# A light convolution with a maxout layer on one core: the chunk with the partitions' first tokens goes last, and the opening's weight work is laid out anew

## The chip, the cores and the metric

The kernel runs on one core of a Trainium2 chip. The metric is the device time of one execution in microseconds (us), taken as the median of several runs. The engines are called as the profile calls them: PE is TensorE's matrix multiply and PEld its loading of weights, DVE is VectorE, ACT is ScalarE, POOL is GpSimd, SP is SyncE, which issues most of the DMA transfers. L802 is line 802 of the kernel's file; the kernel before and the changed one have line numbers of their own.

## The reference

Eight sequences of 4160 tokens with 192 channels are convolved along the sequence. Each token has its own seven taps for each of eight heads of 24 channels; the taps go through a softmax first. The sequence is padded with six zero rows at its front. Then each of the 33,280 tokens goes through a maxout layer of 768 features and back to 192 channels.

```
w = exp(weight_gen - max(weight_gen)); w = w / (sum(w) + 1e-9)          # over the 7 taps
conv[b, s, head, g] = sum over k of w[b, s, head, k] * x_pad[b, s + k, head, g]
h = maximum(maximum(conv @ w1, conv @ w2), conv @ w3)                   # 192 -> 768
out = h @ w_out                                                          # 768 -> 192
```

The four weight matrices arrive as 64-bit floats, the rest is 32-bit.

## The kernel before, in words

**Layout.** The 33,280 tokens lie on 128 partitions, 260 consecutive tokens to each, 16 partitions to a sequence. A *chunk* is four tokens of every partition, 512 tokens, so there are 65 chunks. Chunks are loaded in *supers*: chunk 0 alone, then pairs (1, 2), (3, 4) and so on. A super brings two pieces: the taps `wt` and the tokens `xt`, which have six more tokens ahead of the first one for the convolution; each of the two has two buffers. Those six lie in the same partition's row of the input, except at a partition's first tokens, where they are the last of the partition before, or zeros at a sequence's start. So `load_super` treats the supers with a partition's first six tokens (chunk 0, and chunk 1 with two of them) in another way: a memset of zeros on DVE and eight short transfers, one for each sequence (L305, half of chunk 0's on ACT's queue).

**A chunk's way.** *Softmax* of the taps, once per super: maximum (DVE, L326), difference (POOL, L331), exponential (ACT, L335), sum (DVE, L340), 1e-9 added (DVE, L344), reciprocal (DVE, L348), product (POOL, L352). *Taps*: for each of the four tokens of a partition one product of 128 x 1344 elements on POOL (L370, into one of three buffers `r`) and one sum over the seven taps on DVE (L382, into `acc`). *Turn*: channels must come to the partitions; for chunks 0 and 1 PE transposes (L402, L403), for the later ones DVE transposes 32 x 32 blocks (L421) and 24 ACT copies put them in place (L432). *Parts*: each value is split in a rounded high part and the rest, and the products of the parts together come near 32-bit precision (`xa_hi` L444 and `xc` L449 on ACT, `xa_lo` L460 and `xb` L465 on POOL, for the first two chunks on DVE).

**Products.** The maximum of three is taken as conv @ w1 plus the maximum of 0, conv @ (w2 - w1) and conv @ (w3 - w1). So a chunk has twelve *groups up* (six blocks of 128 features, two differences each), nine matmuls of 64 rows each (L802), and four *groups down* with 30 matmuls each (also L802). Groups down multiply by w_out and, for the w1 term, by w1 @ w_out (`wca`, `wcb`), which `compose` makes once from turned pieces of w1 (`turn_weights` L731 and L733; `compose` L750). Each group has a lower and an upper half of PE's rows; after the last matmul of a lower half an empty instruction stands in SP's queue (L808), and the upper half of that group starts only after it.

**Weights.** `single` makes 32-bit floats out of the 64-bit words in five passes, one on ACT (L573) and four on DVE (L579, L586, L595, L604), the first into a PSUM bank. It does so fifteen times, for nine pieces of 256 elements per partition and six of 384. `prepare_a` and `prepare_b` then take the differences (POOL, L631 and L661), their high parts (ACT) and low parts (POOL, L643 and L673); `prepare_down` does the like for w_out.

**The order.** All instructions are put in order by `Plan` when the program is built, and each engine runs its instructions in that order (`pin`). A task has an engine, a cost, things that must be done before it, buffers that it holds (`holds`, counted against each pool) and a due time. The plan plays the program through: when an engine is free, the ready task with the earliest due time goes next if its buffers are free. Only PE's two queues, L and U, keep the order in which they were written. The due times before are set by hand:

```
    def needed(c):
        return FIRST + PERIOD * c
    ...
        due = needed(cs[0]) - 40
```

The loop writes the chunks in order: twelve groups up of a chunk, with the groups down of the chunk before in the middle; `compose` comes after the first six groups up of chunk 1, and the turns of w1 after chunk 0's groups up.

Of the kernel before, what the change touches and what calls it, by code (L numbers as in the profile page):

```python
# [17 lines left out]
P = 128  # L18


class Hold:


    def __init__(self, pool):
        self.pool, self.users, self.taken, self.tile = pool, 0, False, None


class Task:
    def __init__(self, engine, cost, emit, deps, due, holds, end):
# [11 lines left out]
class Plan:  # L41
# [4 lines left out]
    LATENCY = 0.12  # L46

    def __init__(self, pools):
        self.free = dict(pools)
        self.waiting = {"L": [], "U": []}  # L50
        self.tasks = []

    def add(self, engine, cost, emit, deps=(), due=0.0, holds=(), end=None):
# [3 lines left out]
        if engine in self.FIXED:  # L57
            self.waiting[engine].append(t)
        return t

    def order(self):
        ready, busy, events, done = {}, {}, [], []
        at = dict.fromkeys(self.FIXED, 0)
        for t in self.tasks:
            ready.setdefault(t.engine, [])
            busy.setdefault(t.engine, 0.0)
            if t.missing == 0 and t.engine not in self.FIXED:
                heapq.heappush(ready[t.engine], (t.due, t.n, t))

        def can(t):  # L70
            need = {}
            for h in t.holds:
                if not h.taken:
                    need[h.pool] = need.get(h.pool, 0) + 1
            return all(self.free[p] >= n for p, n in need.items())

        def start(t, now):
            for h in t.holds:
                if not h.taken:
                    h.taken = True  # L80
                    self.free[h.pool] -= 1
# [3 lines left out]
            heapq.heappush(events, (now + t.cost, 0, t.n, t, "free"))  # L85
            heapq.heappush(events, (now + t.end, 1, t.n, t, "given"))
            heapq.heappush(events, (now + t.end + self.LATENCY, 2, t.n, t, "seen"))

        now = 0.0
        while True:  # L90
            for e in ready:
                if busy[e] > now + 1e-9:
                    continue
                if e in self.FIXED:
                    k = at[e]
                    if k < len(self.waiting[e]):
                        t = self.waiting[e][k]
# [33 lines left out]
def lightconv_maxout_kernel(  # L131
# [31 lines left out]
    ON_POOL = (1, 4)  # L163

# [15 lines left out]
    halves = (slice(0, DB), slice(DB, P))  # L180

# [9 lines left out]
    w1a = const.tile([P, NJ, P], F32, name="w1a")  # L191
    b32 = const.tile([P, NP, 3, P], F32, name="b32")
# [39 lines left out]
    plan = Plan(counts | {"conv": 3})  # L232
# [14 lines left out]
    def vec(n):  # L247
        return 0.15 + 0.00105 * n

    def act(n):  # L250
        return 0.18 + 0.00084 * n

    def gps(n):
        return 0.1 + 0.0024 * n


    PERIOD = 21.0
    FIRST = 22.0
# [14 lines left out]
    def load_super(s):  # L273
        cs = supers[s]
        a, n = cs[0] * TC, len(cs) * TC
        hx, hw = xts[s], wts[s] = hold("xt"), hold("wt")
        due = needed(cs[0]) - 40

# [753 lines left out]
```

## Time and profile before

| | |
|---|---|
| median of 3 runs | 1444.12 us (1441.09 to 1446.23) |
| the profiled execution | 1444.6 us |
| its span on the core | 1442.8 us |
| PE busy | 1402.0 us, 97% of the span |
| ACT busy | 1117.3 us, 77% |
| POOL busy | 1104.2 us, 77% |
| DVE busy | 1043.4 us, 72% |
| mean granted PE clock | 0.987 |
| moved by DMA | 85.08 MB, 59 GB/s on the mean |

The shares are means over the whole span, and the stages differ: in the first slices PE is busy for 2 to 8 tenths, then for 9 or more to the end. What a change in the opening is worth is thus read from the opening's own rows (busy time by stretch, what each instruction waited for), and what it does to the rest from a stretch of the rest. A row of the chain of waits gives the start and the length of an instruction, its engine, line, operation, output and inputs, and in brackets how long the engine had waited for it and for what. A row of a group gives the count, the busy time, the mean length in ns and the idle time ahead of it with what ended most of it.

### The profile page before, as it was taken

The numbers are of one execution on the slowest core, as the hardware profiler recorded it, in microseconds if no ns is written. First come the engines' busy times: TensorE is split into PE (matmuls) and PEld (weight loads), VectorE is DVE, ScalarE is ACT, GpSimd is POOL, SyncE is SP. The second block draws the span as 40 slices with busy tenths as digits, with TensorE's granted clock in tenths as the row PEclk, the third lists the DMA queues.
The fourth block names the chain that finished last, engine by engine and source line by source line (L and its number), as shares of the span: only waits on it lengthen the run. The fifth ranks groups of instructions, "written<-read, shape, count | busy, mean of one in ns | idle before, by whom it ended". The sixth has DMA issues, their size and how long they took to land.

```text
span 1442.8 us, 37119 instructions
## 1 busy us (share of the span) xinstructions
PE 1402.0 (97%) x14878; PEld 1366.1 (95%) x14878; DVE 1043.4 (72%) x1433; ACT 1117.3 (77%) x2828; POOL 1104.2 (77%) x609
## 2 busy tenths in 40 slices
PE   2889999999999999999999999999999999999999
PEld 1579999999999999999999999999999999999998
DVE  7867777777777787777778777877877677777543
ACT  3547878878877887787788778877888887788773
POOL 6769888778877887887788778778877877787421
PEclk9679999999999999999999999999999999999999
DMA  7102111111111111111011111101111111110000
GB/s 249 46 1 79 57 68 57 68 68 57 68 46 46 57 68 68 68 57 64 28 57 68 68 68 57 68 25 67 57 68 68 57 68 44 48 57 24 23 21 26
DMA packets 23405, 85.08 MB, mean 59 GB/s; under 512 B 2768, under 2 KB 9544, under 8 KB 19136
## 3 DMA queue, kind: packets, MB, share of 16 engines
q1 hardware_dynamic: 23112, 82.44, 15.5%
q8 instruction: 116, 1.90, 0.5%
q14 instruction: 57, 0.47, 0.1%
q10 hardware_dynamic: 120, 0.28, 0.1%
HBM read 57.15 MB, written 25.56 MB: 57 GB/s over the span
## 4 chain that ended last, share of the span: by engine, by line
PE 95%; POOL 1%; DMA 1%; ACT 1%; SPq 1%; DVE 1%; issue 0%; POOLq 0%
PE bank L802 95%; POOL r L370 1%; DMA xt<-in_x_dram 1%; SPq L532 1%; DVE den L344 0%; ACT room L432 0%; DMA raw<-in_moe_w_dram 0%; SPq L516 0%; PE bank L733 0%; ACT m L859 0%; POOL wa_lo L643 0%; PE bank L731 0%; ACT wb_hi L684 0%; DVE acc L382 0%; ACT bank L573 0%
## 5 line engine op out<-in xcount | busy, mean ns | idle before, releaser
L370 POOL TENSOR_TENSOR r<-xt,wt 128x1344 f32<-128x1344 f32 x260 | 727.1, 2845 | 143.2 <-DVE acc L382 142.9
L802 PE MATMUL bank<-wo,h_hi 64*128 64x384 f32 x3120 | 675.0, 357 | 0.0
L802 PE MATMUL bank<-wo,h_lo 64*128 64x192 f32 x3120 | 603.4, 249 | 0.0
L432 ACT COPY room<-room 32x128 f32<-32x128 f32 x1512 | 448.4, 297 | 79.0 <-DVE room L421 55.9
L802 PEld LDWEIGHTS bank<-wo,h_lo 64*128 64x128 f32 x3120 | 493.0, 188 | 0.0
L802 PEld LDWEIGHTS bank<-wo,h_hi 64*128 64x128 f32 x3120 | 489.2, 186 | 0.0
L802 PE MATMUL bank<-xa_hi,wa_hi 64*128 64x512 f32 x1560 | 479.9, 394 | 6.0 <-ACT wa_hi L637 3.4
L802 PE MATMUL bank<-xa_hi,wa_lo 64*128 64x512 f32 x1560 | 477.9, 390 | 3.4 <-POOL wa_lo L643 3.3
L802 PE MATMUL bank<-xa_lo,wa_hi 64*128 64x512 f32 x1560 | 476.8, 391 | 0.5 <-DVE xa_lo L460 0.5
L382 DVE TENSOR_REDUCE acc<-r 128x192 f32<-128x1344 f32 x260 | 399.8, 1538 | 0.6 <-POOL r L370 0.3
L859 ACT ACTIVATE m<-bank 128x512 f32<-128x512 f32 x390 | 234.5, 601 | 71.4 <-PE bank L802 66.7
L935 DVE TENSOR_TENSOR o<-bank,ob 128x192 f32<-128x192 f32 x260 | 92.4, 356 | 268.7 <-ACT ob L928 268.5
L802 PE MATMUL bank<-xb,wb_hi 64*128 64x512 f32 x780 | 284.5, 390 | 0.3 <-DVE xb L465 0.3
L802 PE MATMUL bank<-xc,wb_hi 64*128 64x512 f32 x780 | 281.1, 390 | 0.2 <-ACT wb_hi L684 0.2
L802 PEld LDWEIGHTS bank<-xa_hi,wa_hi 64*128 64x128 f32 x1560 | 255.3, 186 | 13.5 <-ACT wa_hi L637 4.3
L802 PEld LDWEIGHTS bank<-xa_hi,wa_lo 64*128 64x128 f32 x1560 | 255.3, 186 | 11.2 <-POOL wa_lo L643 5.6
L802 PEld LDWEIGHTS bank<-xa_lo,wa_hi 64*128 64x128 f32 x1560 | 254.9, 187 | 6.4 <-DVE xa_lo L460 1.5
L802 PE MATMUL bank<-xc,wb_lo 64*128 64x512 f32 x780 | 258.0, 389 | 0.0
L867 DVE TENSOR_TENSOR bank<-bank,m 128x512 f32<-128x512 f32 x260 | 179.0, 689 | 42.2 <-PE bank L802 24.3
L878 POOL TENSOR_TENSOR h_lo<-m,h_hi 128x512 fp32r<-128x512 f32 x130 | 171.7, 1321 | 40.0 <-ACT h_hi L871 39.9
L802 PE MATMUL bank<-wca,xa_hi 64*128 64x384 f32 x520 | 183.4, 353 | 0.0
L878 DVE TENSOR_TENSOR h_lo<-bank,h_hi 128x512 fp32r<-128x512 f32 x260 | 172.4, 681 | 11.4 <-ACT h_hi L871 11.2
(79 smaller groups left out, 2012.5 us busy)
## 6 DMA issues: line engine op xcount, KB each, us to landing
xt<-in_x_dram SPq DMA_DIRECT2D x31, 1344.0 KB, 5.8
out_dram<-o SPq DMA_DIRECT2D x64, 384.0 KB, 2.3
wt<-in_weight_gen_dram SPq DMA_DIRECT2D x32, 224.0 KB, 2.6
h_hi<-in_moe_w_dram SPq DMA_DIRECT2D x6, 256.0 KB, 2.9
xt<-in_x_dram SPq DMA_DIRECT2D x1, 1152.0 KB, 5.8
h_lo<-in_moe_w_dram SPq DMA_DIRECT2D x6, 128.0 KB, 4.0
raw<-in_moe_w_dram SPq DMA_DIRECT2D x3, 256.0 KB, 3.6
room<-in_moe_w_out_dram SPq DMA_DIRECT2D x2, 384.0 KB, 6.4
```

The lines of the kernel that those rows point to most:

```text
L370: nc.gpsimd.tensor_tensor(buf(hr).rearrange("p (h g) k -> p k h g", g=G), buf(hx)[:, la + t : la + t + K].rearrange("p k (h g) -> p k h g" ...
L382: pin(nc.vector.tensor_reduce(buf(ha)[:, t], buf(hr), axis=AX.X, op=ALU.add))
L432: pin(nc.scalar.copy(to[:, :, p : p + 32], b[p : p + 32, :, f : f + 32]))
L532: nc.sync.dma_start(out=raw_b()[h, jps[0] : jps[-1] + 1, i].rearrange("p j n w -> p j (n w)"), in_=w[P:].rearrange("p (j o n) -> p j o n", ...
L802: ins = nc.tensor.matmul(buf(hb)[:, :n], w()[h], v()[h], start=half == 0 and first, stop=half == 1 and last,)
L859: lambda: pin(nc.scalar.activation(buf(hm), buf(hb), AF.Relu)), [made], due,
L867: lambda: pin(nc.vector.tensor_tensor(buf(keep), buf(hb), buf(hm), op=ALU.max)),
L878: eng.tensor_tensor(buf(hl)[:, j], buf(keep), buf(hh)[:, j].bitcast(F32), op=ALU.subtract)
L935: nc.vector.tensor_tensor(buf(ho)[:, t], buf(hb)[:, :D], buf(hq), op=ALU.add)
```

## The change: what it does

**The chunk order.** A table `place` says which tokens position c of the program works on: positions 0 to 62 take chunks 2 to 64, and the last two take chunks 0 and 1. The partitions' first tokens are thus in the last super. Their border rows come by four strided transfers (L357) in place of eight per super.

**The opening.** A list `OPENING` writes out loads, softmax, conversions, taps, turns, differences, groups up, compose and groups down for the first two positions; from position 2 on the loop is as before. On PE's queue all turns of both positions' tokens and of w1 now stand ahead of the first group up, and groups of both positions alternate; compose comes after six groups.

**Engines of the weight work.** A table `MODE` says per difference whether POOL or PE makes it (a product with the identity less one with w1, "L") and which engine takes the low part. Both differences of a piece may be one instruction. Ten of the fifteen clamps of `single` go from DVE to POOL, into one of the buffers `m`.

**Single steps.** Two of the first eight tap products go from POOL to DVE; for positions 0 and 1 POOL makes the low parts of h of three blocks of six, not of two; the 1e-9 of every softmax is added on ACT.

**The plan.** Due times may be left out; each task then gets the latest start that the tasks after it allow (`start_by`). Costs are fitted anew, and at most eight transfers are in flight at a time. Loads, softmax and taps from the third super on keep due times, now counted from PE's planned clock.

```diff
+    def start_by(self):
+        for t in reversed(self.tasks):
+            latest = [a.by - self.LATENCY - t.end for a in t.after]
+            if t.due is not None:
+                latest.append(t.due)
+            t.by = min(latest, default=1e6)
...
+    ON_POOL_FIRST = (1, 2, 4)
+    TAPS_ON_VECTOR = ((0, 2), (1, 2))
+    MODE = {
+        ("a", 0): ("POOL", "POOL"),
+        ("a", 1): ("L", "DVE"),
+        ("a", 2): ("POOL", "DVE"),
+        ("b", 0): ("POOL", "POOL"),
+        ("b", 1): ("POOL", "POOL"),
+        ("b", 2): ("POOL", "DVE"),
+    }
+    CLAMP_ON_POOL = (("a", 0, 1), ("a", 1, 1), ("a", 1, 2), ("a", 2, 0), ("a", 2, 1), ("b", 0), ("b", 1), ("b", 2), ("d", 0), ("d", 2),)
...
+    place = [*range(2, NC), 0, 1]
...
+    OPENING = (
+        ("load", 0), ("load a", 0), ("load b",), ("load a", 1), ("load", 1), ("load a", 2),
+        ("load down",), ("softmax", 0), ("softmax", 1), ("singles", 0), ("singles", 1),
+        ("singles", 2), ("singles down",), ("taps", 0), ("taps", 1), ("turn x", 0, 0),
...
+        ("a", 2, 0, 2), ("b", 1), ("b", 2), ("turn", 2), ("parts", 1), ("b", 0), ("up", 0, 0),
+        ("up", 0, 5), ("up", 1, 0), ("compose",), ("up", 0, 2), ("up", 1, 1), ("up", 0, 4),
+        ("up", 0, 1), ("up", 0, 3), ("up", 1, 5), ("up", 1, 4), ("down", 0), ("up", 1, 2),
+        ("up", 1, 3),
+    )
...
-    plan = Plan(counts | {"conv": 3})
+    plan = Plan(counts | {"conv": 3, "flight": 8})
...
-        a, n = cs[0] * TC, len(cs) * TC
+        a, n = place[cs[0]] * TC, len(cs) * TC
...
-        due = needed(cs[0]) - 40
+        due = clock[0] - 31 if s > 1 else LOAD_DUE["s", s]
...
+            step = 2
+            while step <= PB:
+                def rows(step=step):
+                    to = buf(hx)[step // 2 :: step, :z]
+                    of = xf[step // 2 - 1 :: step, NT - z :][: P // step]
+                    pin(nc.sync.dma_start(out=to, in_=of))
...
         e = plan.add(
-            "DVE", 0.3, lambda: pin(nc.vector.tensor_scalar_add(part(hd), part(hd), 1e-9)),
-            [d], due + 3, [hd],
+            "ACT", 0.25,
+            lambda: pin(nc.scalar.activation(part(hd), part(hd), AF.Copy, bias=1e-9)),
+            [d], due(3), [hd],
...
+            eng, cost = ("DVE", vec(D * K)) if (c, t) in TAPS_ON_VECTOR else ("POOL", 2.6)
...
+    def difference(shape, w, of, deps, holds, on):
...
+        def mult():
+            wide = buf(hb)[:, : n * m]
+            pin(nc.tensor.matmul(wide, ident, w().rearrange("p i n -> p (i n)"), start=True, stop=False))
+            for i in range(n):
+                pin(nc.tensor.matmul(wide[:, i * m : (i + 1) * m], minus, of(), start=False, stop=i == n - 1))
```

The order of the instructions on three engines shows where this puts them. The names in it are the buffers with their number; "waits" names the semaphores of an instruction by the engine or the DMA queue that raises them.

SP's queue in the opening, before, from the first transfer of w_out (`room`) to the first store of results:

```order
L552 DMA room_236<-in_moe_w_out_dram 128x2x384 [waits DMAHW1_49]
L552 DMA room_236<-in_moe_w_out_dram 128x2x384 [waits DMAHW2_49]
L552 DMA h_lo_156<-in_moe_w_out_dram 128x2x384 [waits DMAHW3_49]
L280 DMA wt_248<-in_weight_gen_dram 128x448 [waits DMAHW4_49,Pool_49]
L285 DMA xt_250<-in_x_dram 128x2688 [waits DMAHW5_49]
L280 DMA wt_570<-in_weight_gen_dram 128x448 [waits PE_49,DMAHW6_49,Pool_49]
L285 DMA xt_576<-in_x_dram 128x2688 [waits DMAHW7_49]
L949 DMA out_0_dram<-o_852 128x768 [waits PE_49,DMAHW0_49,DVE_49]
```

and the same piece in the changed kernel, where `xt_212` is the second super's tokens, `xt_136` the last super's and `xt_580` the third super's:

```order
L604 DMA room_207<-in_moe_w_out_dram 128x2x384 [waits DMAHW2_49]
L337 DMA xt_212<-in_x_dram 128x2688 [waits DMAHW3_49,Pool_49]
L604 DMA room_207<-in_moe_w_out_dram 128x2x384 [waits DMAHW4_49]
L604 DMA h_lo_155<-in_moe_w_out_dram 128x2x384 [waits DMAHW5_49]
L332 DMA wt_224<-in_weight_gen_dram 128x448 [waits DMAHW6_49]
L339 DMA xt_136<-in_x_dram 128x1536 [waits DMAHW7_49]
L357 DMA xt_136<-in_x_dram 64x1152 [waits DMAHW0_49]
L357 DMA xt_136<-in_x_dram 32x1152 [waits DMAHW1_49]
L357 DMA xt_136<-in_x_dram 16x1152 [waits DMAHW2_49]
L357 DMA xt_136<-in_x_dram 8x1152 [waits DMAHW3_49]
L337 DMA xt_580<-in_x_dram 128x2688 [waits PE_49,DMAHW4_49,Pool_49]
L332 DMA wt_588<-in_weight_gen_dram 128x448 [waits DMAHW5_49]
```

The last super's tokens and their border rows stand in the opening, and the transfers of the second and third super's tokens now wait for POOL, which before only the taps' transfers did.

DVE from the program's start to the first sums over taps, before (L382 is the sum):

```order
L295 MEMSET xt_135 128x1152
L295 MEMSET xt_140 128x384
L326 TENSOR_REDUCE red_150<-wt_133 128x32 [waits DMAHW0_49]
L340 TENSOR_REDUCE den_158<-wt_133 128x32 [waits Activation_49]
L344 TENSOR_SCALAR den_158<-den_158 128x32 [waits DVE_49]
L579 TENSOR_SCALAR bank_161<-bank_161 128x256 [waits Activation_49]
L348 RECIPROCAL den_158<-den_158 128x32 [waits DVE_49]
```

and in the changed kernel (L422 is the product over taps, L434 the sum):

```order
L348 MEMSET xt_136 128x1152
L376 TENSOR_REDUCE red_147<-wt_134 128x32 [waits DMAHW0_49]
L633 TENSOR_SCALAR bank_153<-bank_153 128x256 [waits Activation_49]
L390 TENSOR_REDUCE den_159<-wt_134 128x32 [waits Activation_49]
L639 TENSOR_SCALAR bank_153<-bank_153 128x256 [waits DVE_49]
L648 SCALAR_TENSOR_TENSOR bank_153<-h_hi_138,bank_153 128x256 [waits DMAHW1_49,DVE_49]
L399 RECIPROCAL den_159<-den_159 128x32 [waits Activation_49]
L657 SCALAR_TENSOR_TENSOR w1a_66<-h_hi_138,bank_153 128x256 [waits DVE_49]
L422 TENSOR_TENSOR r_170<-xt_140,wt_134 128x7x192 [waits DMAHW2_49,Pool_49]
L434 TENSOR_REDUCE acc_175<-r_170 128x192 [waits DVE_49]
L434 TENSOR_REDUCE acc_175<-r_168 128x192 [waits Pool_49]
```

The memset of `xt_136`, the last super's buffer, is DVE's first instruction; the 1e-9 is gone from DVE, and a product over taps stands there.

PE ahead of the first group up, before (L402 turns tokens, L802 is the first group):

```order
L402 MATMUL bank_208<-ident_58,acc_201 128x128 [waits DVE_49]
L403 MATMUL bank_210<-ident_58,acc_201 64x128
L802 MATMUL bank_277<-xa_hi_271,wa_hi_59 128x512 [waits Activation_49]
L802 MATMUL bank_277<-xa_lo_282,wa_hi_59 128x512 [waits DVE_49]
L802 MATMUL bank_277<-xc_275,wb_hi_61 128x512 [waits Activation_49]
```

and in the changed kernel, where L825 and L827 turn w1, L455 and L456 turn the second position's tokens and L896 is the first group (first position):

```order
L825 MATMUL bank_349<-ident_58,w1a_66 128x128 [waits PE_49]
L827 MATMUL bank_349<-ident_58,b32_68 128x64 x2
L455 MATMUL bank_300<-ident_58,acc_292 128x128 [waits DVE_49]
L456 MATMUL bank_302<-ident_58,acc_292 64x128
L825 MATMUL bank_375<-ident_58,w1a_66 128x128 [waits DVE_49]
L827 MATMUL bank_375<-ident_58,b32_68 128x64 x2
L825 MATMUL bank_387<-ident_58,w1a_66 128x128 [waits DVE_49]
L827 MATMUL bank_387<-ident_58,b32_68 128x64 x2
L896 MATMUL bank_397<-xa_hi_232,wa_hi_59 128x512 [waits PE_49,Activation_49]
```

The first group up followed the first position's own turns; now the last turn of the second position's tokens and the last of w1 stand ahead of it.

More of the change, by code (lines that the diff above doesn't have):

```diff
@@ L608, in single, with whole, singles @@
             ),
-            [d], due, [hb, hc, *holds],
+            [d], None, [hb, hc, *holds],
         )
     w_hi, w_lo, b_hi, b_lo, one_a, one_b = {}, {}, {}, {}, {}, {}
-    def prepare_a(jp):
+    of_bank = {}
+    def whole(cost, emit, deps, holds):
+        got = plan.add(
+            "L", cost, emit, [*deps, made, *u_last()], clock[0], holds, end=cost + 0.25
+        )
+        clock[0] += cost
+        return got
+    def singles(jp):
         pair = slice(2 * jp, 2 * jp + 2)
@@ new lines, in difference, with rest, differences_a @@
+        return lambda: buf(hb)[:, : n * m].rearrange("p (i n) -> p i n", i=n), d, [hb]
+    def rest(size, to, of, hi, deps, holds, on):
+        eng = nc.gpsimd if on == "POOL" else nc.vector
+        return plan.add(
+            on, gps(size) if on == "POOL" else vec(size),
+            lambda: pin(eng.tensor_tensor(to(), of(), hi(), op=ALU.subtract)), deps, None, holds,
+        )
+    def differences_a(jp, first, last):
+        pair = slice(2 * jp, 2 * jp + 2)
+        hx, got = of_bank["x", jp]
+        on, then = MODE["a", jp]
+        n = last - first
+        v, d, holds = difference(
+            (n, 2 * P), lambda: buf(hx)[:, first:last],
+            lambda: w1a[:, pair].rearrange("p j n -> p (j n)"), [*got[first:last], one_a[jp]],
+            [hx], on,
+        )
+        of = lambda: v().rearrange("p i (j n) -> p i j n", j=2)
+        place_of = lambda w: w[:, pair, first:last].rearrange("p j i n -> p i j n")
+        hi = plan.add(
+            "ACT", act(2 * n * P), lambda: pin(nc.scalar.copy(place_of(wa_hi), of())), [d], None,
+            holds,
+        )
+        lo = rest(
+            2 * n * P, lambda: place_of(wa_lo), of, lambda: place_of(wa_hi).bitcast(F32), [hi],
+            holds, then,
+        )
+        for i in range(first, last):
+            w_hi[jp, i], w_lo[jp, i] = hi, lo
@@ new lines, in lightconv_maxout_kernel @@
+    step = {
+        "load": load_super, "load a": load_a, "load b": load_b, "load down": load_down,
+        "softmax": softmax, "singles": singles, "singles down": singles_down, "taps": opening_taps,
+        "turn x": turn_tokens, "parts": opening_parts,
+        "a": differences_a, "b": differences_b, "up": ups,
+        "turn": turn_weights, "compose": compose, "down": downs,
+    }
+    for what, *which in OPENING:
+        step[what](*which)
+    for c in range(2, NC):
+        s = super_of[c]
+        if s > 1 and supers[s][0] == c:
+            load_super(s)
+            softmax(s)
+        tokens(c)
+        for j in range(DOWN_AT):
+            ups(c, j)
+        if c < NC - 1:
+            downs(c - 1)
+        for j in range(DOWN_AT, NJ):
+            ups(c, j)
```

393 lines of the change are left out of this document (186 added, 207 removed).

## The prediction

> **What bounds the kernel now.** I read first the stretches of the span (length; then busy time and instruction count of PE, PEld, DVE, ACT and POOL; granted PE clock; DMA share; GB/s):
>
> ```profile
> 0.00:20.00 20.00, 1.38 (x4) 0.47 (x4) 11.33 (x23) 3.29 (x6) 12.85 (x13) 1.00 0.64 196
> 20.00:40.00 20.00, 12.26 (x39) 8.04 (x40) 18.13 (x36) 8.81 (x21) 15.60 (x15) 1.00 0.76 254
> 40.00:60.00 20.00, 14.97 (x57) 10.26 (x57) 16.21 (x30) 11.77 (x27) 18.94 (x15) 0.67 0.01 1
> 60.00:80.00 20.00, 19.21 (x88) 14.42 (x87) 12.58 (x18) 12.14 (x32) 10.24 (x8) 0.65 0.21 81
> 80.00:100.00 20.00, 14.78 (x85) 13.70 (x84) 14.03 (x13) 5.75 (x16) 17.09 (x8) 0.78 0.00 1
> 400.00:800.00 400.00, 400.00 (x4364) 394.45 (x4362) 298.42 (x402) 325.85 (x829) 322.23 (x173) 1.00 0.16 57
> ```
>
> From 400 to 800 us PE never idles: 4364 matmuls in 400 us, so the 228 of a chunk (108 for its twelve groups up, 120 for its four groups down) take 20.90 us. In the first 100 us it does 273, while DVE and POOL are busy almost throughout. Next, rows of the chain of waits in order of time, of the copies that follow the last groups down, of PE's groups before 92.2 us and of PE's waits:
>
> ```profile
> 92.22 1347.23 PE bank L802 x12536
> 1426.63 0.32 ACT L928 COPY ob<-bank 128x192 f32<-128x192 f32 x1 [1.84 <-PE bank L802]
> 1439.47 0.32 ACT L928 COPY ob<-bank 128x192 f32<-128x192 f32 x1 [1.82 <-PE bank L802]
> L802 PE MATMUL bank<-xa_hi,wa_lo 64*128 64x512 f32 x36 | 18.0, 544 | 3.4 <-POOL wa_lo L643 3.3
> PE bank L402 <- DVE acc L382: 21.8, 4, 16.6
> PE bank L802 <- DVE wcb L767: 5.2, 1, 5.2
> ```
>
> From 92.22 us to the end the chain is PE alone. A group down costs (1439.47 - 1426.63) / 6 = 2.14 us, so a group up costs (20.90 - 4 x 2.14) / 12 = 1.03 us. Before 92.22 us 36 matmuls of one kind ran, two to a group: 18 groups up, 18.5 us of work. So some 74 us of the opening are not products, and only these can be won; the rest moves with PE's rate.
>
> The profiled time is 92.2 + 1347.2 + 3.4 (from the last product to the end) = 1442.8 us of span, and 1.8 us around it, 1444.6 us; the median of the runs is 0.5 us lower.
>
> **The change part by part.** Call T0 the moment at which compose (the 24 matmuls of w1 with w_out) ends. After it the new order has no weight work on PE; six groups up are done by then, against 18 at 92.22 us, so 12 x 1.03 = 12.4 us of products are owed. New time = T0 + 12.4 + 1347.2 + 3.4 + stalls + 1.8. The sum is now about T0. Rows for prices (start us, duration us; where rows follow without a wait, start to start is the price):
>
> ```profile
> 2.82 0.39 DVE L326 TENSOR_REDUCE red<-wt 128x32 f32<-128x224 f32 x1 [0.34 <-DMA wt<-in_weight_gen_dram]
> 5.30 1.28 ACT L335 ACT_TABLE_LOAD   x1 [5.30 <-DMA xt<-in_x_dram]
> 9.01 10.23 POOL L370 TENSOR_TENSOR r<-xt,wt 128x1344 f32<-128x1344 f32 x4
> 36.51 0.73 POOL L631 TENSOR_TENSOR wx<-wx,w1a 128x256 f32<-128x256 f32 x1
> 37.20 0.73 POOL L661 TENSOR_TENSOR b<-b 128x256 f32<-128x256 f32 x1
> 34.32 0.42 DVE L579 TENSOR_SCALAR bank<-bank 128x256 f32<-128x256 f32 x1
> 34.65 0.42 DVE L595 SCALAR_TENSOR_TENSOR bank<-h_hi,bank 128x256 uint32<-128x256 uint32 x1
> 57.07 0.56 DVE L579 TENSOR_SCALAR bank<-bank 128x384 f32<-128x384 f32 x1
> 57.54 0.55 DVE L604 SCALAR_TENSOR_TENSOR wo<-room,bank 128x384 uint32<-128x384 uint32 x1
> 58.47 1.54 DVE L382 TENSOR_REDUCE acc<-r 128x192 f32<-128x1344 f32 x1
> 59.92 0.55 DVE L595 SCALAR_TENSOR_TENSOR bank<-h_lo,bank 128x384 uint32<-128x384 uint32 x1
> 82.37 4.17 PE L750 MATMUL bank<-wo,raw 128*128 128x192 f32 x24
> 25.00:30.00 5.00, 3.04 (x7) 1.62 (x9) 4.97 (x13) 4.34 (x11) 4.79 (x5) 1.00 0.98 297
> ```
>
> POOL: a tap 2.56 us, a 256-wide pass 0.69. DVE: 0.33 at 256, 0.47 at 384, 1.45 for a reduce. DMA: 297 KB per us at its fullest, and the first transfer is there at 2.8 us.
>
> *The first tokens.* With them last, sixteen border transfers (four of them ACT's) leave the start; ACT's table load waited behind its own until 5.30 us. Without that the softmax of the first chunk is done near 7 us, and its 0.98 MB of tokens, behind 0.38 MB, land at 1.36 MB / 297 KB per us + 2.8 = 7.4. First tap at 7.5 instead of 9.01. The four border transfers of the last super fall where DMA is nearly idle (share 0.01 from 40 us on).
>
> *The second super's tokens.* The memset for the last super is free to run at once, and takes one of the two xt buffers until the end. So xt_212 is loaded only when the taps of chunk 0 are done. Three are on POOL: 7.5 + 3 x 2.56 = 15.2 us. Ahead of it stand 5.3 MB (nine pieces of 262 KB, six of 197, the rest tokens, taps' weights and w_out), 18 us; with its own 1.38 MB (4.6 us) and the 2.8 us it lands near 25.5, and hardly later if it is issued at 19. SP is held meanwhile; behind it wait two pieces of w_out, which land near 28 and are read by DVE only after 40.
>
> *Chunk 1.* PE's order puts all turns of both chunks and all weights ahead of the first product, so chunk 1's taps are on the path. On POOL: three taps, two clamps (0.69 at 256 wide, 1.0 at 384) and then six 256-wide passes, 7.7 + 1.7 + 4.1 = 13.5 us, so 39 us. ACT must cast the pair whose difference is made on PE behind chunk 1's first turn, and the work queued behind that cast on ACT adds about 2: **first product at 41**. Clamps on POOL occur in no row; bounds are DVE's 0.33 and the 1.3 us of POOL's 512-wide passes, and I take the two-input pass of the same width, the nearest. The tap on DVE occurs in no row either. Lower bound: DVE's own pass over 1344 elements, 1.45. For the upper bound:
>
> ```profile
> 75.67 0.20 DVE L344 TENSOR_SCALAR den<-den 128x64 f32<-128x64 f32 x1
> 87.79 4.12 DVE L344 TENSOR_SCALAR den<-den 128x64 f32<-128x64 f32 x1
> 84.07 7.80 POOL L370 TENSOR_TENSOR r<-xt,wt 128x1344 f32<-128x1344 f32 x3
> ```
>
> The same DVE instruction takes 0.20 us alone and 4.12 beside three taps on POOL: it ends when they do (91.87). So the DVE tap may wait until POOL pauses, 2 taps and 2 clamps, 6.8 us; then the third POOL tap, which needs the buffer of a reduce, follows the DVE tap and two reduces (4.4), and the rest is as above: 25.5 + 6.8 + 4.4 + 2.6 + 4.1 + 2 = 45.4, with DVE's queue in between **47**. I take the late end, the nearest row being one in which DVE did wait. Moving the +1e-9 from DVE to ACT removes this wait later on, where it costs nothing but DVE's own time.
>
> The Trainium skill, SBUF — State Buffer, section on SBUF's two separate sides, says that VectorE and GpSimd share a port pair as an exclusive lock for a whole instruction, and counts a VectorE operation with two SBUF inputs among those that need it. By it the late end holds for both moved taps; and the sum is 1430; if only two-port modes took the lock, the early one, 1424. The 4.12 us row agrees for a one-input operation; no row here shows one with two.
>
> *To T0.* Six groups up follow. PE comes from idling:
>
> ```profile
> 45.00:50.00 5.00, 5.00 (x23) 4.20 (x23) 1.21 (x4) 3.92 (x10) 4.52 (x5) 0.50 0.01 2
> 63.06 0.54 DVE L604 SCALAR_TENSOR_TENSOR wo<-h_lo,bank 128x384 uint32<-128x384 uint32 x1
> ```
>
> At a granted clock of 0.50 it did 23 matmuls in 5 us, so the first two groups (18) cost 3.9 us, not 2.1. Then the third pair's weights and, on DVE, the three conversions of w_out: some 24 operations of 0.33 to 0.60 us, 11.5 us after chunk 1's last reduce (38.5 us early, 44 late), so 50 or 55.5, about 1.5 more for the products between them. DVE was 91% busy from 20 to 40 us, so it cannot go much faster. The last pair of groups and compose (4.17 us) end at **T0 = 56 early, 62 late**. The difference made on PE for one pair lies in PE's idle time there, at the price of three wide matmuls if PE were busy. The new costs and deadlines in the planner run nothing themselves; they act through these places alone.
>
> *After T0.* Eighteen groups up and four down (18.5 + 8.6 = 27 us) cover the tapping of chunks 2 and 3; the single xt buffer makes this tight. Stalls: 0 to 8 us, 4 taken, somewhat below the one 5.2 us wait that PE had there before.
>
> 62 + 12.4 + 1347.2 + 3.4 + 4 + 1.8 = 1430.8, less 0.5 to the median: **1430 us**. Early end without stalls 1420; with one more 4.12 us wait and 8 us of stalls, 1438.
>
> *The steady state.* POOL's work for two chunks, against PE's 41.8 us:
>
> ```profile
> L370 POOL TENSOR_TENSOR r<-xt,wt 128x1344 f32<-128x1344 f32 x260 | 727.1, 2845 | 143.2 <-DVE acc L382 142.9
> L878 POOL TENSOR_TENSOR h_lo<-m,h_hi 128x512 fp32r<-128x512 f32 x130 | 171.7, 1321 | 40.0 <-ACT h_hi L871 39.9
> L460 POOL TENSOR_TENSOR xa_lo<-room,xa_hi 128x512 fp32r<-128x512 f32 x63 | 81.7, 1297 | 66.1 <-ACT xa_hi L444 62.5 <-PE bank L802 1.3
> L465 POOL TENSOR_TENSOR xb<-room,xc 64x512 fp32r<-64x512 f32 x63 | 81.2, 1288 | 22.4 <-PE bank L802 22.2
> L331 POOL TENSOR_TENSOR wt<-wt,red 128x448 f32<-128x448 f32 (+1 forms) x33 | 33.4, 1012 | 9.6 <-DVE red L326 8.2 <-issue 1.4
> L352 POOL TENSOR_TENSOR wt<-wt,den 128x448 f32<-128x448 f32 (+1 forms) x33 | 31.8, 965 | 31.2 <-DVE den L348 31.2
> xt<-in_x_dram SPq DMA_DIRECT2D x31, 1344.0 KB, 5.8
> 1011.57 2.84 POOL L370 TENSOR_TENSOR r<-xt,wt 128x1344 f32<-128x1344 f32 x1 [3.19 <-DVE acc L382]
> 29.83 0.29 PEld L802 LDWEIGHTS bank<-xa_hi,wa_hi 64*128 64x128 f32 x2 [0.81 <-SPq L808]
> ```
>
> Eight taps 22.8, four h_lo 5.3, xa_lo and xb of two chunks 5.2, two softmax passes 2.0: 35.2 us. A load that no longer runs ahead adds at most 5.8, and in the new order two h_lo passes (2.6) stand in that gap, so 38.4 of 41.8. I count nothing for it.
>
> **The rivals.**
>
> 1. *DVE's work stays the bound.* Its fifteen conversions ended at 63.6 us before (the row above); the change takes ten clamps off it (about 4 us) and gives it two taps and three subtractions (about 4.5 us). If the last conversion of w_out again ends near 63, compose ends at 68 and the time is 1430 + 6 = 1436. For: DVE's busy share. Against: its load is the same but starts earlier, and chunk 2's first passes no longer stand among it.
> 2. *The gain goes in the refill.* xt_580 and the next two loads wait for POOL's last tap of a super, with PE's products behind. Two landings of 5.8 us uncovered and T0 at 66: 1430 + 4 + 11.6 - 4 = 1442, no change that can be told. Against: six groups and chunk 0's groups down cover the first.
> 3. *One xt buffer slows every super* (the slower side). The load stands in SP's queue among the nops for which PE's upper half waits (0.81 us in the row above); while SP waits for POOL's last tap, these nops are late. POOL's cycle is 35.2 + 5.8 = 41.0 if nothing covers the load, and it waited 3.19 us for a reduce in the row above; from 0.8 us of such waits per super PE loses time. With half of that wait, 1.6 us, the cycle is 42.6: 0.8 us x 31 supers = 25 us, 1455. Against: the two h_lo passes in the gap.
>
> A measurement of this kernel tells 0.3% (4.3 us) from no change.
>
> **How the numbers follow.** Forecast 0.64, rival 1 0.14, rival 2 0.10, rival 3 0.12. Forecast and rival 1 count as faster, less 0.01: 0.77. Rival 2 with that is no change, 0.11; rival 3 slower, 0.12. The range goes from 1420, T0 early without a stall, past rival 1 to 1441, where rival 2 begins; the forecast's own is 1420 to 1438.
>
> **What will show it.** In the chain of waits a stretch of PE alone from about 60 us instead of 92; the first product between 41 and 47; compose's 24 matmuls ending between 56 and 62; the xt landing of the second super near 25; DVE taps of 1.5 us or of more than 5; in the stretch from 400 to 800 about 4364 matmuls again. I am wrong if that count falls (rival 3), if PE idles for more than 8 us between T0 and 200 us (rival 2), or if compose ends after 66 (rival 1).

## The result, and the profile after

The change makes the kernel slower: 1512.66 us (median of 4 runs, 1510.97 to 1513.5) against 1443.96 us (4 runs) on the same chip, a ratio of 1.0475 with a 95% interval of 1.0454 to 1.0496. The prediction was 1430 us, with 1441 as its upper end.

The stretches of the changed kernel's span, with the columns as in the prediction:

```profile
0.00:20.00 20.00, 2.88 (x9) 1.28 (x9) 15.59 (x23) 5.08 (x12) 13.02 (x13) 1.00 0.94 294
20.00:40.00 20.00, 6.45 (x24) 3.92 (x23) 19.56 (x31) 6.04 (x16) 16.57 (x16) 1.00 0.40 156
40.00:60.00 20.00, 17.78 (x90) 14.57 (x90) 18.07 (x32) 15.55 (x38) 16.68 (x14) 0.74 0.00 1
60.00:80.00 20.00, 18.43 (x151) 17.06 (x150) 11.70 (x18) 15.76 (x41) 10.86 (x10) 0.94 0.22 82
80.00:100.00 20.00, 20.00 (x217) 18.93 (x216) 12.80 (x18) 8.90 (x18) 18.86 (x10) 0.97 0.06 21
400.00:800.00 400.00, 384.04 (x4040) 359.58 (x4038) 271.31 (x364) 304.65 (x785) 301.92 (x161) 1.00 0.15 55
```

The opening won what was forecast: PE has done 484 matmuls by 100 us, against 265 before (the rows add up to 491 and 273, since a matmul that crosses an edge stands in both). The loss lies in the rest. From 400 to 800 us PE does 4040 matmuls where it did 4364, 30 us' worth in 400; PEld is idle for 40 us of them, where it was for 6. The first group up and compose, from PE's timeline, show the opening's two marks (start, length):

```profile
44.61 0.79 PE L896 MATMUL bank<-xa_hi,wa_hi 64*128 64x512 f32 x1 [0.55 <-ACT raw L832]
55.20 4.17 PE L844 MATMUL bank<-wo,raw 128*128 128x192 f32 x24
```

Compose ends at 59.4 us. With the prediction's terms the span without a loss would be 59.4 + 12.4 + 1347.2 + 3.4 = 1422.4 us; it is 1510.5, so 88 us went after the opening, 2.8 us for each of 31 supers.

The chain that ended last was PE for 95% of the span before. Now it runs through all engines:

```profile
ACT 27%; POOL 24%; PE 22%; issue 17%; DVE 9%; DMA 0%; ACTq 0%; POOLq 0%; SPq 0%; DVEq 0%
```

And PE's waits on parts of h (us in total, times, longest), with three rows of the half of PE that has begun a chunk's groups down:

```profile
PE bank L896 <- ACT h_hi L965: 22.0, 26, 1.3
PE bank L896 <- DVE h_lo L972: 14.4, 47, 0.9
639.38 0.28 PE L896 MATMUL bank<-wo,h_lo 64*128 64x192 f32 x1
640.49 0.44 PE L896 MATMUL bank<-wo,h_hi 64*128 64x384 f32 x1 [0.82 <-ACT h_hi L965]
641.21 0.35 PE L896 MATMUL bank<-wo,h_lo 64*128 64x192 f32 x1 [0.23 <-DVE h_lo L972]
```

From 639.38 to 641.21 us the group down gets on by two matmuls; at the old rate (4364 in 400 us, in two halves) a half starts one each 0.18 us. Groups down need the high part of h (ACT) and the low part (DVE or POOL) of all six blocks, and the last of them come too late. Before, PE never idled ahead of them (0.0 us in these matmuls' rows). The two waits add up to 36 us of the 88. The same list has 34.5 and 28.2 us for PEld on the same parts, partly at the same time, so it doesn't divide up the whole loss.

### The profile page after: what moved, and what is told of

It reads as the page before. It is cut to its first block, busy times and chain, and to the rows that moved or that the text cites. A ratio compares the mean times of both kernels' runs of the same rounds, so it can differ in the third digit from the quotient of the medians.

```text
span 1510.5 us, 37015 instructions
## 1 busy us (share of the span) xinstructions
PE 1424.0 (94%) x14884; PEld 1332.6 (88%) x14884; DVE 1023.5 (68%) x1392; ACT 1117.7 (74%) x2860; POOL 1106.5 (73%) x611
## 4 chain that ended last, share of the span: by engine, by line
ACT 27%; POOL 24%; PE 22%; issue 17%; DVE 9%; DMA 0%; ACTq 0%; POOLq 0%; SPq 0%; DVEq 0%
PE bank L896 22%; ACT room L491 15%; POOL r L422 9%; ACT h_hi L965 6%; ACT m L953 5%; POOL h_lo L972 5%; POOL xb L523 4%; POOL xa_lo L518 4%; DVE room L480 3%; DVE acc L434 3%; DVE m L961 1%; POOL wt L403 1%; DVE bank L961 1%; DVE h_lo L972 0%; PE bank L844 0%
## 5 line engine op out<-in xcount | busy, mean ns | idle before, releaser
L422 POOL TENSOR_TENSOR r<-xt,wt 128x1344 f32<-128x1344 f32 x258 | 718.8, 2843 | 66.9 <-DVE acc L434 62.0
L896 PE MATMUL bank<-wo,h_hi 64*128 64x384 f32 x3120 | 669.9, 357 | 22.1 <-ACT h_hi L965 22.0
L896 PE MATMUL bank<-wo,h_lo 64*128 64x192 f32 x3120 | 602.0, 250 | 10.7 <-DVE h_lo L972 9.9
L491 ACT COPY room<-room 32x128 f32<-32x128 f32 x1512 | 448.3, 297 | 124.8 <-DVE room L480 103.5
L896 PEld LDWEIGHTS bank<-wo,h_lo 64*128 64x128 f32 x3120 | 491.6, 188 | 25.6 <-DVE h_lo L972 21.8
L896 PEld LDWEIGHTS bank<-wo,h_hi 64*128 64x128 f32 x3120 | 482.6, 185 | 28.2 <-ACT h_hi L965 28.2
L896 PE MATMUL bank<-xa_hi,wa_hi 64*128 64x512 f32 x1560 | 499.4, 398 | 8.2 <-DVE h_lo L972 4.5
L896 PE MATMUL bank<-xa_lo,wa_hi 64*128 64x512 f32 x1560 | 492.5, 392 | 4.9 <-POOL xa_lo L518 4.9
L896 PE MATMUL bank<-xa_hi,wa_lo 64*128 64x512 f32 x1560 | 486.6, 389 | 0.0
L434 DVE TENSOR_REDUCE acc<-r 128x192 f32<-128x1344 f32 x260 | 400.5, 1543 | 23.7 <-POOL r L422 22.7
L896 PE MATMUL bank<-xc,wb_hi 64*128 64x512 f32 x780 | 294.0, 389 | 0.0
L896 PEld LDWEIGHTS bank<-xa_hi,wa_hi 64*128 64x128 f32 x1560 | 256.3, 185 | 32.4 <-DVE h_lo L972 12.7
L896 PE MATMUL bank<-xb,wb_hi 64*128 64x512 f32 x780 | 277.1, 391 | 4.5 <-POOL xb L523 4.3
L896 PE MATMUL bank<-xc,wb_lo 64*128 64x512 f32 x780 | 269.2, 388 | 0.0
L896 PEld LDWEIGHTS bank<-xa_lo,wa_hi 64*128 64x128 f32 x1560 | 254.3, 185 | 15.7 <-POOL xa_lo L518 7.9
L896 PEld LDWEIGHTS bank<-xa_hi,wa_lo 64*128 64x128 f32 x1560 | 255.1, 185 | 9.3
L972 DVE TENSOR_TENSOR h_lo<-bank,h_hi 128x512 fp32r<-128x512 f32 x258 | 176.4, 685 | 99.7 <-ACT h_hi L965 98.8
L896 PE MATMUL bank<-wca,xa_hi 64*128 64x384 f32 x520 | 183.6, 354 | 0.2 <-SPq L902 0.2
```

The lines of the kernel that those rows point to most:

```text
L422: on.tensor_tensor(buf(hr).rearrange("p (h g) k -> p k h g", g=G), buf(hx)[:, la + t : la + t + K].rearrange("p k (h g) -> p k h g", g=G), ...
L434: pin(nc.vector.tensor_reduce(buf(ha)[:, t], buf(hr), axis=AX.X, op=ALU.add))
L491: pin(nc.scalar.copy(to[:, :, p : p + 32], b[p : p + 32, :, f : f + 32]))
L896: ins = nc.tensor.matmul(buf(hb)[:, :n], w()[h], v()[h], start=half == 0 and first, stop=half == 1 and last,)
L972: eng.tensor_tensor(buf(hl)[:, j], buf(keep), buf(hh)[:, j].bitcast(F32), op=ALU.subtract)
```

## The experiments

The ratios are against the kernel before on the same chip.

| kernel | us | ratio to before, 95% | matmuls 400 to 800 us |
|---|---|---|---|
| before (four medians) | 1441.9 to 1444.0 | | 4364 |
| the change | 1512.7 | 1.0475 (1.0454, 1.0496) | 4040 |
| late_zero: change, two buffers xt for most supers | 1509.8 | 1.0466 (1.0450, 1.0482) | 4120 |
| three_xt: change, three buffers xt | 1502.3 | 1.0413 (1.0392, 1.0434) | 4106 |
| before_place: before, chunk order alone | 1475.1 | 1.0221 (1.0200, 1.0242) | 4229 |
| hlo4: change, one low part of h per chunk on POOL | 1475.8 | 1.0230 (1.0209, 1.0251) | 4212 |
| lz_act: late_zero, ACT's old costs in the plan | 1434.5 | 0.9950 (0.9934, 0.9965) | 4372 |
| lz_m30: late_zero, old cost of the 24 copies only | 1457.4 | 1.0107 (1.0085, 1.0129) | 4296 |
| be_m207: before, new cost of the 24 copies | 1493.7 | 1.0359 (1.0337, 1.0381) | 4214 |
| **af_act: change, ACT's old costs in the plan** | **1426.8** | **0.9898 (0.9880, 0.9915)** | 4355 |
| bp_dma: before_place, new cost of a load | 1450.3 | 1.0046 (1.0030, 1.0063) | 4350 |
| af_taps: af_act, all taps on POOL | 1432.8 | 0.9927 (0.9904, 0.9951) | 4363 |
| af_clamp: af_act, all clamps on DVE | 1434.9 | 0.9943 (0.9922, 0.9966) | 4364 |
| af_all: af_act, old costs of DVE and POOL too | 1429.8 | 0.9910 (0.9882, 0.9937) | 4346 |

### The buffer that is held from the start

The first theory was the prediction's third rival: the memset for the last super takes one of two buffers xt for the whole run, so each load waits for POOL's last tap. Two kernels give the buffer back, one takes it from the old kernel, and one changes what stands in the gap.

```diff
 # late_zero: in the plan alone, the memset comes after a late group
-    "DVE", 1.1, lambda: pin(nc.vector.memset(buf(hx)[:, :z], 0.0)), (), due, [hx]
+    "DVE", 1.1, lambda: pin(nc.vector.memset(buf(hx)[:, :z], 0.0)), last_upper[-24:-23], due, [hx]
 # three_xt
-    "xt": 2
+    "xt": 3
 # before_place: to the kernel before
+    place = [*range(2, NC), 0, 1]
-    a, n = cs[0] * TC, len(cs) * TC
+    a, n = place[cs[0]] * TC, len(cs) * TC
-        a = c * TC
+        a = place[c] * TC
 # hlo4
-    ON_POOL = (1, 4)
+    ON_POOL = (4,)
```

> The changed kernel, but in the plan the memset of zeros for the last super comes only after a group some 24 groups ahead of that super's end of writing, so that the second buffer xt stays in use for all other supers. Theory A (the held buffer makes the loss: each super's tokens are loaded only after POOL's last tap of the super before): from 400 to 800 us PE does about 4360 matmuls again, the opening keeps its gain (compose ends near 59 us), and the time is 1444.6 - 20.5 = 1424 us, 1418 to 1430. Theory B (the plan's new costs and due times give POOL a worse order, whatever the buffers): about 4050 matmuls from 400 to 800 us and 1490 us or more.

> The changed kernel with three buffers xt in place of two; the memset of the last super stays first on DVE and holds one of the three. Theory A: two buffers are left for the rest, about 4360 matmuls from 400 to 800 us, 1418 to 1430 us. Theory B: 1490 us or more.

> The kernel before with one part of the change alone: the chunk order with the partitions' first tokens last. Its old plan, costs and due times stay, and by them too the memset for the last super's buffer is DVE's first instruction. Theory A: the loss comes with it, 2.9 us for each of 31 supers, about 1444 + 90 = 1534 us less a gain of a few us in the opening, 1500 to 1540, and 4000 to 4150 matmuls from 400 to 800 us. Theory B: the old plan keeps its rate, 4360 matmuls and 1435 to 1450 us.

> The changed kernel with its one buffer left, but from the third chunk on POOL makes one low part of h per chunk (block 4) and not two; the other (block 1) goes to DVE. So no low part that waits for the next chunk's products stands between POOL's last tap of a super and the first of the next. Theory A1 (the load is a fixed piece of POOL's round, about 32.6 us of work + 3.2 of waits + 4.8 of uncovered load = 40.6 us, under PE's 41.8): near PE's rate, 4250 to 4360 matmuls from 400 to 800 us and 1425 to 1455 us, since the 7 us gap of the changed kernel is longer than the load only by the wait for that low part. Theory A2 (the exposed load costs by itself, through the queues behind it, whatever stands in the gap): 1490 us or more.

Theory A fell. With two buffers back in use the kernel is nearly as slow as without the edit (1509.8 and 1502.3 us); in late_zero:

```profile
400.00:800.00 400.00, 388.80 (x4120) 376.17 (x4118) 281.30 (x371) 312.03 (x795) 303.95 (x163) 0.99 0.16 56
```

But the old plan does lose 33 us by the chunk order alone, between the ranges of the two theories, and there POOL waits for the tokens 28 times, 131.7 us in all (in the changed kernel once, 2.8 us):

```profile
615.30 2.81 POOL L371 TENSOR_TENSOR r<-xt,wt 128x1344 f32<-128x1344 f32 x1 [4.70 <-DMA xt<-in_x_dram]
```

hlo4 fits neither of its theories; it removes some of the loss, and which part of it was not settled. So something in the new plan itself costs, with one buffer or two.

### What the plan believes of ACT

late_zero has the same buffers as the kernel before, so the order of its engines can be laid beside the old one. On ACT it differs: all 24 copies that put a chunk's turned tokens in place (L432 before, L491 in the changed kernel) stand ahead of the last high parts of h, where the old order left six of them for the time of the groups down. Two lines of the diff, which the excerpt above left out, say why:

```diff
     def act(n):
-        return 0.18 + 0.00084 * n
+        return 0.08 + 0.00083 * n
 ...
-                got.append(plan.add("ACT", 0.296, move, [turned], due - 11 + q, [hv]))
+                got.append(plan.add("ACT", 0.207, move, [turned], clock[0] - 2 + q, [hv]))
```

The groups of the profile before had the true lengths (mean ns behind the comma):

```profile
L432 ACT COPY room<-room 32x128 f32<-32x128 f32 x1512 | 448.4, 297 | 79.0 <-DVE room L421 55.9
L859 ACT ACTIVATE m<-bank 128x512 f32<-128x512 f32 x390 | 234.5, 601 | 71.4 <-PE bank L802 66.7
L871 ACT CAST h_hi<-bank 128x512 fp32r<-128x512 f32 x260 | 146.2, 585 | 8.0 <-DVE bank L867 5.6
```

A copy takes 297 ns, not 207. An instruction over 512 elements takes 601 or 585, where the new formula gives 505. For a chunk that is 24 x 0.09 = 2.2 us for the copies and 6 x 0.096 + 6 x 0.08 = 1.1 us for relu and high parts, 3.3 us at least that the plan believes free. ACT had 325.85 us of work in 400, 17.0 of the 20.90 us of a chunk, so 3.9 us are free in truth.

The Trainium skill, VectorE: DVE Perf Modes, section on the TRN2 errata, gives ScalarE 224 cycles plus the elements of a partition, divided by the factor of a perf mode if there is one, from SBUF to SBUF, at 1.2 GHz. Without such a factor that is an estimate of 293 ns for a copy of 128 elements. The row of 297 ns agrees; 207 does not.

```diff
 # lz_act (on late_zero) and af_act (on the change)
-        return 0.08 + 0.00083 * n
+        return 0.18 + 0.00084 * n
-    plan.add("ACT", 0.207, move,
+    plan.add("ACT", 0.296, move,
 # lz_m30 (on late_zero)
-    plan.add("ACT", 0.207, move,
+    plan.add("ACT", 0.3, move,
 # be_m207 (on the kernel before)
-    plan.add("ACT", 0.296, move,
+    plan.add("ACT", 0.207, move,
```

> The changed kernel with the memset of the last super late (two buffers xt in use) and, beside that, the plan's costs of ACT as before: 0.296 us for one of the 24 copies that turn a chunk's tokens in place of 0.207, and 0.18 + 0.00084 n in place of 0.08 + 0.00083 n for the rest. The plan's other costs and all due times are the changed ones. Theory C (by the short costs the plan puts all 24 copies of the next chunk ahead of the last high parts of h, so ACT ends these late, and PE's groups down wait for them, 2.1 us per super): six of the 24 copies stand behind the first copy of a group down again, no such waits on PE, about 4360 matmuls from 400 to 800 us, 1424 us (1418 to 1432). Theory D (the backward due times and the other costs make the loss): 1480 us or more.

> As lz_act, but only the cost of the 24 copies is mended (0.3 us); 0.08 + 0.00083 n stays for ACT's other work. Theory C: the plan then leaves two to three of the 24 copies behind the last high parts, so part of the loss of 2.1 us per super is gone: 1424 to 1470 us, 4230 to 4360 matmuls from 400 to 800 us. Theory D: 1480 us or more.

> The kernel before with one number changed: the plan's cost of one of the 24 copies is 0.207 us in place of 0.296. Theory C: nearly all 24 copies stand ahead of the last high parts of h, and groups down wait about 2 us per super: 1480 to 1515 us, 4100 to 4200 matmuls from 400 to 800 us. Theory D: unchanged, 1436 to 1450 us and 4360 matmuls.

> The changed kernel with ACT's costs in the plan as before (as in lz_act), but with the last super's memset first on DVE as in the change, so that one buffer xt is left. Theory C with the price of one buffer as the old plan pays it (33 us between the kernel before and the same with the chunk order alone): 1424 + 33 = 1457 us, 1445 to 1480. If the buffer costs nothing once ACT is in order: 1424 us. Theory D: 1500 us or more.

Theory C holds, from both sides. One number in the old kernel (be_m207) costs 52 us. ACT's rows around the first copies of results (`ob`), in the kernel before:

```profile
622.74 0.62 ACT L871 CAST h_hi<-m 128x512 fp32r<-128x512 f32 x1
...
624.26 0.30 ACT L928 COPY ob<-bank 128x192 f32<-128x192 f32 x1
624.59 1.84 ACT L432 COPY room<-room 32x128 f32<-32x128 f32 x6
626.46 0.32 ACT L928 COPY ob<-bank 128x192 f32<-128x192 f32 x1
```

and in be_m207:

```profile
596.15 1.83 ACT L432 COPY room<-room 32x128 f32<-32x128 f32 x6
...
598.50 0.92 ACT L432 COPY room<-room 32x128 f32<-32x128 f32 x3
599.44 0.62 ACT L871 CAST h_hi<-m 128x512 fp32r<-128x512 f32 x1
...
600.57 0.30 ACT L432 COPY room<-room 32x128 f32<-32x128 f32 x1
600.89 0.32 ACT L928 COPY ob<-bank 128x192 f32<-128x192 f32 x1
602.06 0.32 ACT L928 COPY ob<-bank 128x192 f32<-128x192 f32 x1 [0.85 <-PE bank L802]
```

Before, six copies fill the 1.84 us between two results. In be_m207 they stand earlier, among the relus and high parts: 23 of the chunk's 24 are ahead of its last high part, where it was 17. Nothing is left for the time between the results, and ACT idles there. PE, which before had no such wait, waits 26 times for a low part that DVE makes from such a high part, 21.2 us in all. The changed kernel has the same picture: copies (L491) between the high parts (L965), for which PE waits at 640.49 us above:

```profile
632.64 0.30 ACT L491 COPY room<-room 32x128 f32<-32x128 f32 x1 [3.90 <-DVE room L480]
...
633.34 0.56 ACT L965 CAST h_hi<-bank 128x512 fp32r<-128x512 f32 x1
633.92 1.53 ACT L491 COPY room<-room 32x128 f32<-32x128 f32 x5
...
636.10 0.92 ACT L491 COPY room<-room 32x128 f32<-32x128 f32 x3
637.04 0.62 ACT L965 CAST h_hi<-m 128x512 fp32r<-128x512 f32 x1
...
638.91 0.91 ACT L491 COPY room<-room 32x128 f32<-32x128 f32 x3
639.85 0.59 ACT L965 CAST h_hi<-bank 128x512 fp32r<-128x512 f32 x1
```

With ACT's old costs and all else as in the change (af_act), eight copies stand among the results again:

```profile
604.81 0.32 ACT L1022 COPY ob<-bank 128x192 f32<-128x192 f32 x1
605.16 1.85 ACT L491 COPY room<-room 32x128 f32<-32x128 f32 x6
607.03 0.32 ACT L1022 COPY ob<-bank 128x192 f32<-128x192 f32 x1
607.37 0.60 ACT L491 COPY room<-room 32x128 f32<-32x128 f32 x2
```

PE's list has no wait for parts of h any more, its rate is back and the kernel is faster than both, 1426.8 us. The due times of the change are kept in this run, so they were not what cost the time. lz_m30 says how the two costs share the loss on late_zero: the copies' cost alone takes 1509.8 to 1457.4 us, the rest of ACT's formula another 23 us.

lz_act, with two buffers, lies above its expected range and is 8 us slower than af_act with one. Its rate from 400 to 800 us is not lower (4372). It loses near the end:

```profile
1371.10 0.50 PE L897 MATMUL bank<-xa_hi,wa_hi 64*128 64x512 f32 x1 [1.88 <-ACT xa_hi L503]
1372.44 0.79 PE L897 MATMUL bank<-xa_lo,wa_hi 64*128 64x512 f32 x1 [0.85 <-POOL xa_lo L519]
```

Around 1371 us PE waits for parts of the last super's tokens, which that edit brings late; from 1350 to 1380 us it does 233 matmuls, and 336 in af_act, some 9 us' worth. That belongs to the edit and not to the change.

### What one buffer costs

```diff
 # bp_dma (on before_place)
-        w = transfer(0.0005 * n * H * K, weights, (), due, [hw])
+        w = transfer(0.11 * n, weights, (), due, [hw])
-            t = [transfer(0.0005 * (n + PAD) * D, tokens, (), due + 0.1, [hx])]
+            t = [transfer(0.38 * (n + PAD), tokens, (), due + 0.1, [hx])]
```

> The kernel before with the chunk order alone (1475 us, POOL waits 4.7 us per super for the tokens), and with the plan's cost of a load as the change has it (0.38 us per token for xt, 0.11 for wt, where the old plan has 0.096 and 0.22). Theory E (the one buffer costs only because the old plan takes the load for 3.3 us and puts a tap where the tokens are not there yet; with the longer load it fills the gap with low parts of h): 1436 to 1455 us and at least 4320 matmuls from 400 to 800 us. Theory F (with ACT's costs right, one buffer costs 30 us whatever the plan knows of the load): 1468 to 1482 us, about 4230.

Theory E holds: when the plan takes a load of tokens for 7.3 us and not for 3.3 (it lasts 5.8), the old plan gets its rate back (4350) with one buffer, 1450.3 us. The changed kernel's plan already has nearly that cost. So af_act missed its first figure, 1457 us, which put the old plan's price on the buffer, and came near the other, 1424. POOL's rows in af_act, from the low part behind the super's last tap to the next super's first taps:

```profile
598.72 1.35 POOL L972 TENSOR_TENSOR h_lo<-m,h_hi 128x512 fp32r<-128x512 f32 x1
603.45 1.29 POOL L972 TENSOR_TENSOR h_lo<-m,h_hi 128x512 fp32r<-128x512 f32 x1 [3.38 <-ACT h_hi L965]
605.08 5.50 POOL L422 TENSOR_TENSOR r<-xt,wt 128x1344 f32<-128x1344 f32 x2 [0.33 <-DMA xt<-in_x_dram]
```

Two low parts of h stand in the gap and the taps start 0.33 us after the wait for the load began. In the changed kernel the same gap is longer, and not by the load:

```profile
613.93 1.29 POOL L972 TENSOR_TENSOR h_lo<-m,h_hi 128x512 fp32r<-128x512 f32 x1
622.27 1.29 POOL L972 TENSOR_TENSOR h_lo<-m,h_hi 128x512 fp32r<-128x512 f32 x1 [7.05 <-ACT h_hi L965]
623.53 5.50 POOL L422 TENSOR_TENSOR r<-xt,wt 128x1344 f32<-128x1344 f32 x2
```

### Two terms of the opening, and the other costs

```diff
 # all three on af_act: af_taps
-    TAPS_ON_VECTOR = ((0, 2), (1, 2))
+    TAPS_ON_VECTOR = ()
 # af_clamp
-    CLAMP_ON_POOL = (("a", 0, 1), ...)
+    CLAMP_ON_POOL = ()
 # af_all: vec, gps, the tap, its sum and the transposition cost what they did before
```

> af_act (the changed kernel with ACT's costs in the plan as before, 1426.8 us) with all eight first tap products on POOL. In the changed kernel's trace the two products on DVE take 2.58 and 3.33 us, and the POOL product beside the first 4.88 us in place of 2.62. Theory G (the two engines take turns, so a product on DVE spares POOL nothing): 1424 to 1429 us. Theory H (each saves a POOL product of 2.6 us on the path to the first group): 1429.5 to 1433 us.

> af_act with all fifteen clamps on DVE. Theory I (DVE bounds the opening, as rival 1 of the prediction had it, so ten clamps of 0.33 to 0.47 us more on DVE move compose by their sum): 1429 to 1432 us. Theory J (the path runs over the second chunk's taps and ACT, the clamps lie beside it): 1425 to 1428 us.

> af_act with the plan's costs of DVE, POOL, taps, sums and the 32 x 32 transposition as before, too. If only ACT's costs were wrong, nothing more is won or lost: 1422 to 1432 us, about 4360 matmuls from 400 to 800 us. If the other short costs hurt as well, the order gets better: below 1422 us.

af_act's first group starts at 44.25 us and its compose at 55.22. The same two rows in af_taps and in af_clamp:

```profile
43.95 0.79 PE L896 MATMUL bank<-xa_hi,wa_hi 64*128 64x512 f32 x1 [1.61 <-DVE xb L523]
64.51 4.17 PE L844 MATMUL bank<-wo,raw 128*128 128x192 f32 x24
```

```profile
50.42 0.77 PE L896 MATMUL bank<-xa_hi,wa_hi 64*128 64x512 f32 x1
60.41 4.17 PE L844 MATMUL bank<-wo,raw 128*128 128x192 f32 x24
```

By the ratios (0.9927 and 0.9943 to af_act's 0.9898) taps back on POOL cost about 4 us, clamps back on DVE about 6.5. The intervals of af_taps and af_act overlap, so the 4 us are not clear of noise. The taps' time is on Theory H's side, but not by its way: the first group starts no later, and compose 9 us later. The plan had put the rest of the weight work in another order (PE waits 2.61 us at 56.05 for a weight's high part, a wait that af_act doesn't have), so this run doesn't price the taps alone. The clamps' is Theory I's case, somewhat above its sum of 4, with the first group 6.2 us later. af_all (0.9910) can't be told from af_act: DVE's and POOL's new costs did no harm.

## Why the prediction was wrong, point by point

**The step that failed** is one sentence in the part on the change: "The new costs and deadlines in the planner run nothing themselves; they act through these places alone." The places meant were those of the opening. The step put the planner's costs at nothing after T0. In truth the plan's costs set the order of all 65 chunks. An ACT that looks 3.3 us per chunk emptier than it is got the copies of the next chunk ahead of work that PE needs sooner. Between the change and af_act lie 1512.7 - 1426.8 = 86 us (83 by the ratios). For the steady state the prediction took POOL's durations from the trace and added them up, and that sum was right; it made no such sum for ACT, and took the order in which the work runs as given. The row with 297 ns was on the profile's page, the 0.207 in the diff.

**The opening** came out inside its bounds. First tap at 7.0 us (7.5 forecast); the second super's tokens issued at 17.0 and tapped from 24.7 (15 to 19, and 25.5); first group at 44.6 (41 to 47, 47 taken); compose's end at 59.4 (56 to 62, 62 taken). With 12.4 us owed and PE's rate as before, 59.4 + 12.4 + 1347.2 + 3.4 = 1422.4 us, and af_act's span is 1424.9: stalls of 2.5 us, where 4 were taken. That the sum came out so close is in part luck: the trace bears out neither end's account of the tap on DVE, and the terms below were mis-sized.

**Sizes within it.** POOL's clamps were taken at the price of a two-input pass, 0.69 and 1.0 us; they take 0.40 and 0.51:

```profile
17.82 0.40 POOL L633 TENSOR_SCALAR m<-m 128x256 f32<-128x256 f32 x1
20.12 0.51 POOL L633 TENSOR_SCALAR m<-m 128x384 f32<-128x384 f32 x1 [1.90 <-ACT m L628]
```

The taps on DVE, put between 1.45 and 1.45 + 6.8 us, took 2.58 and 3.33. The late end supposed that DVE waits for a pause of POOL, up to 6.8 us; it waited about 1 us, as the last section shows. The four border transfers, which were put where DMA is nearly idle, from 40 us on, were issued from 19.64 to 23.84 us; POOL's taps at 24.70 us don't wait for tokens.

**The steady state with one buffer.** "I count nothing for it" was right once ACT is in order: af_act runs with one buffer at 4355 matmuls. The two low parts of h fill the gap as the prediction said.

**The rivals.** Rival 1, DVE as the opening's bound, was no more than half there: ten clamps more on DVE cost about 6.5 us, but compose ended at 59.4 and not at 68. Rival 2 didn't occur. Rival 3 named the right symptom, a falling count in every super, and the right side, with a price of 25 us for 88. Its cause was wrong: two buffers lose as well (late_zero), and one buffer need not (af_act). It would have come true in the old plan, whose cost of a load is too low (before_place, 33 us).

## What to carry to other kernels

A planner's cost table is part of the program's text: when a change touches it, lay each number beside the mean of that instruction's row in the profile, and add up per engine what is missing in one period, against that engine's true slack. Here 3.3 us were missing of 3.9 free ones, on an engine whose busy share was 77% and which looked harmless. When PE starts to wait in the steady state, compare the order of the engine that it waits for with the old order, ahead of any theory on buffers.

## What the runs showed of the hardware that was not expected

A two-input product over taps on DVE and one on POOL do not run side by side. In the changed kernel's opening:

```profile
7.01 2.58 DVE L422 TENSOR_TENSOR r<-xt,wt 128x1344 f32<-128x1344 f32 x1 [0.41 <-POOL wt L403]
7.06 9.93 POOL L422 TENSOR_TENSOR r<-xt,wt 128x1344 f32<-128x1344 f32 x3
L422 POOL TENSOR_TENSOR r<-xt,wt x6: 2620/2632/4877, 7.1 to 32.8; 128x1344 f32<-128x1344 f32 x6
```

Of POOL's six taps (shortest, median and longest in ns) the longest took 4.88 us beside DVE's of 2.58, 2.25 us more than the median, nearly the whole length of DVE's. By the rows DVE came first, by 0.05 us, and POOL waited; in the kernel before it was DVE whose 0.20 us instruction took 4.12. The second pair begins the other way round:

```profile
24.70 7.33 POOL L422 TENSOR_TENSOR r<-xt,wt 128x1344 f32<-128x1344 f32 x2
26.36 3.33 DVE L422 TENSOR_TENSOR r<-xt,wt 128x1344 f32<-128x1344 f32 x1
```

POOL's first tap here takes 2.63 us and ends at 27.33. DVE's product ends at 29.69, and POOL's second tap, from 27.2 us, takes 4.82. So DVE waited about 1 us for the tap that was running, and then POOL waited for DVE: they took turns. In the kernel before, DVE's instruction began at 87.79 in the second of three taps and let the third, from 89.1 us, pass as well. Why DVE got in between two taps in one case and not in the other no run here shows. The Trainium skill, SBUF — State Buffer, section on SBUF's two separate sides, has it that whichever starts first holds the shared ports for the whole instruction: the rows agree in both directions. Which part of DVE's 2.58 us is its own work no run shows, since none has such a product without POOL beside it.
